# A cap on transfers under way, a planner that charges for instruction pages, and V scaled on VectorE in two groups

## The chip, the core and the metric

One core of a Trainium2 chip runs the whole program. Its engines work side by side, each through its own list of instructions in order: TensorE (PE in the profile; its weight loads are shown apart as PEld), VectorE (DVE), ScalarE (ACT), GpSimd (POOL) and SyncE (SP), which here issues the transfers between device memory and on-chip memory. An engine waits for another at a semaphore. The metric is the device time of one execution in microseconds (us), the median over runs.

## The reference

Two parts follow each other. The first is a delta-rule attention over 4 batches, 8 heads, 768 tokens and 48 dimensions, written token by token; the second is a gated MLP over the 3072 tokens that come out of it.

```python
k_n = k / (norm(k) + 1e-06)
for t in range(S):
    y[:, :, t] = q[:, :, t] @ state
    v_old = k_n[:, :, t] @ state
    state = state + beta[t] * outer(k_n[:, :, t], v[:, :, t] - v_old)
x = y as (3072, 384)
out = (sigmoid(x @ w_gate) * (x @ w_val)) @ w_out      # 384 -> 1536 -> 384
```

All values are float32.

## The kernel before

**Groups.** The 768 tokens are cut into 12 groups g of 64 tokens (all 32 pairs of batch and head at once). Inside a group the recurrence is not run token by token but solved: a Gram matrix of the keys (`gram`, L259), its blocks copied out by ScalarE (L267, L272), norms on VectorE (`norms`, from L208), then a triangular solve on VectorE, a row at a time. Groups 0 and 1 take a shorter solve on two halves (`solve_halves`, L343 and L346), after which TensorE joins the halves with two products of 128 small matmuls each, `pz` and `pm` (`joining`, L375), with a copy of z on ScalarE between them (`keep_z`, L379) and the step T on VectorE behind them (L355). The other groups use the long solve (L311, L314). Then the state's share is taken off V (`less`, L401), the updates are formed (`updates`, L413 and L420, copied by L426 and L428), the output rows (`rows`, L448 and L451) and, from them, the transposed input of the MLP (`flip`, L490; `keep_x`, L496 and L498). The next group's state comes from `advance` (L471, L478, L480). V is first scaled by the key norms, 16 operations of 48 elements on ScalarE for each group (`scale_v`, L247).

**MLP.** For each group and each of 12 blocks f of the hidden dimension there is a gate product of 18 matmuls (`gate_val`, L508), a sigmoid and a product (L513, L518), a split in an upper and a lower half (L523, L528), and an output product of 6 matmuls (`outp`, L544). Group 0 takes blocks 0 to 5 first, then group 1 takes all 12, then group 0 the rest, and after that each group has its 12 in turn.

**Weights.** They come as 36 pieces of 384 KB. Each is converted once: two operations on ScalarE (`tail_bits` L165, `rescale` L170), `join` on VectorE (L182), the upper half on ScalarE (L187) and the lower on VectorE (L192). All stay on the chip. The first six transfers go at once; piece n from 6 on waits for a one-element copy on GpSimd (`mark`, L175) that waits for the conversion of piece n - 6.

**Transfers.** All are issued by SyncE, in the planner's order: keys by dimension (`load_k`, L87), queries (`load_q`, L91), keys and V by token with beta (`load_rows`, L98, L101), pieces (`load_piece`, L155), and the stores of the results.

**The planner.** Every step is a task with an engine, a cost in ns, what it comes after, and the buffers that it takes and frees. `schedule` (from L751) gives each task a level, the longest way from it to the end, and builds the lists by a simulation: the engine that can start earliest takes the ready task of the highest level, with a small slack. Up to the first gate product it fills TensorE's gaps of over 450 ns with warm-up products of zeros (`warm_up`, L201), as many as it expects to fit; they are then fixed in the list. The order that comes out is each engine's program.

Of the kernel before, what the change touches and what calls it, by code (L numbers as in the profile page):

```python
# [14 lines left out]
U32 = mybir.dt.uint32  # L15
# [4 lines left out]
ALU = mybir.AluOpType  # L20
# [10 lines left out]
J = 8  # L31
CP = 2 * J
# [18 lines left out]
NSUB = GT // 128  # L51
EPS = 1e-6
CUT = 6


@with_exitstack
def deltanet_gated_mlp(ctx: ExitStack, tc: tile.TileContext, kd, qd, kv, beta, words, out):
# [24 lines left out]

    state = [{} for _ in range(N)]

    def load_k(g):
        for e in range(2):
            nc.sync.dma_start(kqp[g % 2][64 * e:64 * e + D, 0:2].rearrange("p s c t -> p (s c t)"), kd[g, e])  # L87

    def load_q(g):
        for e in range(2):  # L90
            nc.sync.dma_start(kqp[g % 2][64 * e:64 * e + 64, 2 + e:4 + e].rearrange("p s c t -> p (s c t)"), qd[g, e])  # L91

    def load_rows(g, part):

        st = state[g]
        if "kv" not in st:
            st["kv"] = wk.tile([128, 2, CP, D], F32, name=f"kv_{g}", tag="kv", bufs=2)
        nc.sync.dma_start(st["kv"][:, part].rearrange("p c d -> p (c d)"), kv[g, :, part * CP * D:(part + 1) * CP * D])  # L98
        if part:
            st["beta"] = wk.tile([128, 32], F32, name=f"beta_{g}", tag="beta", bufs=2)  # L100
            nc.sync.dma_start(st["beta"], beta[:, g])  # L101

    def load_group(g):
        load_k(g)
        load_q(g)
        load_rows(g, 1)
        load_rows(g, 0)

    def constants():
        nc.gpsimd.memset(zero, 0.0)  # L110
# [35 lines left out]
    pieces.append((NF - 1, "o"))  # L146
    raw, parts = {}, {}

    AHEAD = 6

    def load_piece(n):
        f, w = pieces[n]
        if n < AHEAD:
            raw[n] = wt.tile([128, PW, 2], U32, name=f"raw_{n}", tag=f"w{n}")
        nc.sync.dma_start(raw[n].rearrange("p c w -> p (c w)"), words[3 * f + "gvo".index(w)])  # L155

    def words_of(n):

# [8 lines left out]
    def rescale(n):  # L167

        h = words_of(n)[2].bitcast(F32)
        nc.scalar.activation(h, h, AF.Prelu, scale=2.0 ** -112, alpha=-2.0 ** 32)  # L170

    def mark(n):

        raw[n] = wt.tile([128, PW, 2], U32, name=f"raw_{n}", tag=f"w{n}")
        nc.gpsimd.tensor_copy(out=raw[n][0:1, 0:1, 0], in_=raw[n - AHEAD][0:1, 0:1, 1])  # L175

    us = {}

# [64 lines left out]

    def scale_v(g):
        V, mq = state[g]["kv"][:, 1], state[g]["mq"]
        for c in range(CP):
            nc.scalar.activation(V[:, c], V[:, c], AF.Copy, scale=mq[:, c, 0:1])  # L247
            yield
# [114 lines left out]
    def joining(g, n):  # L363

        st = state[g]
        if g == 0 and n == "pm":
            st["pm"] = st["pz"]
        else:
            pool, tag = (ps_aux, "aux") if g else (ps_gv, "gv")
            st[n] = pool.tile([128, CP, 32], F32, name=f"{n}_{g}", tag=tag)  # L370
        out = st[n]
        lhsT, rhs = (scratch[:, 0], mt) if n == "pz" else (scratch[:, 1], scratch[:, 2])
        for c in range(CP):
            for r in range(0, 128, 32):
                nc.tensor.matmul(out=out[r:r + 32, c], lhsT=lhsT[r:r + 32, c], rhs=rhs[r:r + 32, c], start=True, stop=True)  # L375

    def keep_z(g):

# [3 lines left out]
    def rest(g):  # L382

        st = state[g]
        kq, V = kqp[g % 2], st["kv"][:, 1]
# [6 lines left out]
        if g == 0:  # L392
            st["R"] = [V[:, e * J:(e + 1) * J] for e in range(2)]
        else:
            st["R"] = [None, None]

    def less(g, e, step):
# [5 lines left out]
    def updates(g, step):  # L403

        st = state[g]
        R, L = st["R"], st["L"]

        at = {(e, x): [tokens_at(e, x) + 32 * (k ^ e) for k in range(2)] for e, x in KINDS}
        if step == 1:
            for j in range(J):  # L410
                for e, x in KINDS:
                    one, two = at[e, x]
                    nc.tensor.matmul(out=st["pk"][e][two:two + 32, j], lhsT=L[one:one + 32, e * J + j], rhs=su[one:one + 32, 3 if x else e, j],  # L413
                                     start=False, stop=True, skip_group_check=True)
            return
        st["pu"] = pu = [ps_aux.tile([128, J, D], F32, name=f"pu_{g}_{step}_{x}", tag="aux") for x in range(1 if g else 2)]
        for j in range(J):
            for e, x in KINDS:
                r = at[e, x][step // 2]
                nc.tensor.matmul(out=pu[0 if g else x][r:r + 32, j], lhsT=mt[r:r + 32, e * J + j], rhs=R[e][r:r + 32, j], start=True, stop=True)  # L420
# [150 lines left out]
        tasks.append(t)  # L571
        return name

    def on_dve(n):
        return 158 + 1.03 * n

    def on_act(n):
        return 165 + 0.85 * n
# [15 lines left out]
    pools = dict(aux=2, seq=2, gv=1, po=2, G=1, gp=1, X=1, mt=1, scratch=1, row=3, ys=1, sg=3, h=3, u=3, kv=2, L=2, xa=0, xb=1, mq=1)  # L594
# [19 lines left out]
    def load(g, what):  # L614
        k = f"kq{g % 2}"
        if what == "k":
            transfer(f"dk{g}", lambda: load_k(g), 2, 1900, has(f"pk{g - 2}", f"pp{g - 2}"))
        if what == "q":
            transfer(f"dq{g}", lambda: load_q(g), 2, 2200, has(f"yy{g - 2}"))
        if what == "v":  # L620
            transfer(f"dv{g}", lambda: load_rows(g, 1), 2, 1350, has(f"pd{g - 2}", f"less{g - 2}.1.1"))
        if what == "t":
            transfer(f"dt{g}", lambda: load_rows(g, 0), 1, 1150, has(f"pd{g - 2}"))

    HALF = {0, 1}

    def recurrence(g):
# [12 lines left out]
        for i in range(4):  # L640
            by = [task(f"sv{g}.{i}", ACT, 1020, lambda: [next(sv, None) for _ in range(4)], by)]
# [32 lines left out]
        r = [f"sv{g}.3"]  # L674
        if g:
            r = [task(f"less{g}.0.{e}", DVE, 555, lambda e=e: less(g, e, 0), [f"pk{g}", f"sv{g}.3"], take=("row",)) for e in range(2)]
        kinds = [(e, x) for e, x in KINDS]
        two = g == 0

# [56 lines left out]

    half = constants()
    second_half(half)
    for n in range(len(pieces)):
        fetch(n)  # L740
        convert(n)
        split(n)
    for g in range(N):
        for what in "kvqt":
            load(g, what)
        recurrence(g)
    for i in range(N * NF):
        tile_of(i)
        out_of(i)

    def schedule():  # L751

# [3 lines left out]
            for a in t["after"]:  # L756
                a["then"].append(t)
        for t in reversed(tasks):
            t["level"] = t["late"] + max([(0 if b["engine"] == t["engine"] else LATENCY[t["engine"]] + t["lands"] + t["load"]) + b["level"] for b in t["then"]] or [0]) + t["cost"]
# [5 lines left out]
        order, between, filling = [], [], [True]  # L765

        def release(t):
            when[t["n"]] = max([a["done"] if a["engine"] == t["engine"] == PE else a["end"] for a in t["after"]] or [0.0])
# [4 lines left out]
        while len(order) < len(tasks):  # L773
# [19 lines left out]
            if e == PE and filling:  # L793
                clock[e] = max(clock[e], READY)
                while at - clock[e] > ROOM:
                    between.append(dict(name="warm", fn=warm_up, start=clock[e], engine=PE, done=clock[e] + FILL))
                    clock[e] += FILL
# [10 lines left out]
            clock[e] = t["done"]  # L808
            for p in t["free"]:
                tokens[p].append(t["end"])  # L810
            ready[e].remove(t)
            order.append(t)
            for b in t["then"]:
# [2 lines left out]
                    release(b)  # L816
        return sorted(order + between, key=lambda t: t["start"])

    READY, FILL, ROOM = 2500, 230, 450
# [51 lines left out]
```

## Time and profile before

| | before |
|---|---|
| Median of 3 runs | 655.1 us (653.84 to 655.85) |
| The profiled execution's own time | 654.68 us |
| Its span, first to last instruction | 652.6 us |
| TensorE busy | 630.2 us (97%) |
| VectorE busy | 475.4 us (73%) |
| ScalarE busy | 323.3 us (50%) |
| GpSimd busy | 16.6 us (3%) |
| Transfers, mean rate | 63 GB/s |

A line of groups names the line, the engine, the operation, what it writes and reads with shapes, and how often it comes; then its busy time and the mean length of one, and after the bar the idle time of the engine just before it and what ended that. "issue" means that the profile shows nothing that the engine waited for. A line of the timeline begins with the start and the length in us. TensorE's matmuls are pipelined, so a sum of lengths can exceed the time. The granted clock of TensorE is a share of its full speed.

### The profile page before, as it was taken

Reading aid. Unit: us, or ns where it says so; the run is one execution under the profiler, and the core shown is the slowest. Engines: PE = TensorE matmul, PEld = TensorE weight load, DVE = VectorE, ACT = ScalarE, POOL = GpSimd, SP = SyncE. Lnnn points to the kernel's source line nnn. Section 1 sums busy time; section 2 is a strip of 40 time slices with the busy share of each in tenths; the row PEclk is TensorE's granted clock in tenths of the full one; section 3 lists DMA queues with packets and bytes.
Section 4 is the critical chain, followed back from the end, with each engine's and each line's share of the span. In section 5 each row is a group of like instructions: output and inputs, shape, how many; then the busy total and the mean of one; then the engine's idle time right before and its main releaser. Section 6 shows DMA issues by size and latency. Waiting matters only on the chain.

```text
span 652.6 us, 24378 instructions
## 1 busy us (share of the span) xinstructions
PE 630.2 (97%) x10618; PEld 591.3 (91%) x10626; DVE 475.4 (73%) x1482; ACT 323.3 (50%) x881; POOL 16.6 (3%) x57
## 2 busy tenths in 40 slices
PE   8785999999999999999999999999999999999996
PEld 5445999989999999999999999999999999999996
DVE  4785799996977976976976976976976986983221
ACT  4867799346355355355345345345345345344321
POOL 5010100000000000000000000000000000000000
PEclk9988999999999999999999999999999999999999
DMA  9858350030211211211211211211211210100101
GB/s 262 267 182 268 110 160 12 2 83 20 58 51 28 58 52 27 58 51 27 59 52 27 58 51 28 59 51 27 58 51 28 59 51 3 27 2 4 25 1 24
DMA packets 17770, 41.08 MB, mean 63 GB/s; under 512 B 4224, under 2 KB 7296, under 8 KB 17664
## 3 DMA queue, kind: packets, MB, share of 16 engines
q1 hardware_dynamic: 17664, 39.53, 21.6%
q8 instruction: 83, 1.36, 0.9%
q14 instruction: 23, 0.19, 0.1%
HBM read 34.80 MB, written 4.72 MB: 61 GB/s over the span
## 4 chain that ended last, share of the span: by engine, by line
PE 85%; DMA 5%; DVE 4%; issue 3%; ACT 1%; SPq 0%; POOL 0%; ACTq 0%; POOLq 0%
PE gv L508 46%; PE po L544 23%; DMA raw<-in_words_dram 3%; PE pu L420 3%; PE yy L448 2%; PE yy L451 2%; PE pp L283 2%; PE pg L259 2%; PE pk L390 2%; PE pk L413 1%; DMA kv<-in_kv_dram 1%; PE pt L490 1%; PE pd L471 1%; DVE X L314 1%; DVE tmp L311 1%
## 5 line engine op out<-in xcount | busy, mean ns | idle before, releaser
L508 PE MATMUL gv<-xx,w 128*128 128x256 f32 x2592 | 333.1, 284 | 1.5 <-DVE sg L518 1.5
L508 PEld LDWEIGHTS gv<-xx,w 128*128 128x128 f32 x2592 | 325.6, 191 | 3.0 <-ACT sg L513 1.1
L544 PE MATMUL po<-w,h 128*128 128x384 f32 x864 | 180.7, 346 | 0.0
L544 PEld LDWEIGHTS po<-w,h 128*128 128x128 f32 x864 | 146.0, 188 | 3.8 <-ACT ot L556 0.2
L513 ACT ACTIVATE sg<-gv 128x256 f32<-128x256 f32 x144 | 54.9, 381 | 151.0 <-PE gv L508 150.7
L518 DVE TENSOR_TENSOR sg<-sg,gv 128x256 f32<-128x256 f32 x144 | 60.0, 416 | 78.8 <-ACT sg L513 78.6
L523 ACT CAST h<-sg 128x256 fp32r<-128x256 f32 x144 | 58.5, 406 | 89.6 <-DVE sg L518 88.9
L314 DVE TENSOR_TENSOR X<-X,tmp 128x126 f32<-128x126 f32 (+22 forms) x310 | 79.0, 255 | 9.1
L311 DVE TENSOR_TENSOR tmp<-X,gp 128x126 f32<-128x126 f32 (+22 forms) x310 | 78.2, 252 | 7.3
L528 DVE TENSOR_TENSOR h<-sg,h 128x256 fp32r<-128x256 f32 x144 | 59.9, 416 | 16.6 <-ACT h L523 15.9
L428 ACT COPY su<-pu 32x384 f32<-32x384 f32 x92 | 43.3, 471 | 23.8 <-PE pu L420 22.7
L247 ACT ACTIVATE kv<-kv,mq 128x48 f32<-128x48 f32 x192 | 46.9, 323 | 3.6 <-DVE mq L241 3.5
L201 PE MATMUL warm<-zero 128*128 128x512 bf16 x114 | 30.1, 420 | 3.9 <-issue 2.8
L288 DVE TENSOR_TENSOR kqp<-pp,pmask 64x512 f32<-64x512 f32 x48 | 32.1, 685 | 2.0 <-PE pp L283 1.7
L267 ACT COPY G<-pg 32x256 f32<-32x256 f32 (+1 forms) x72 | 26.4, 367 | 9.0 <-PE pg L259 5.4
L201 PEld LDWEIGHTS <-zero 128*128 128x128 bf16 x122 | 12.3, 106 | 17.8 <-issue 6.0
L208 DVE STREAM_TRANSPOSE gp<-G 128x1024 f32<-128x1024 f32 x12 | 14.9, 1245 | 16.8 <-ACT G L267 16.8
L401 DVE TENSOR_TENSOR R<-kv,pk 128x384 f32<-128x384 f32 x44 | 22.4, 550 | 3.3 <-PE pk L390 2.1
L192 DVE TENSOR_TENSOR w<-u,w 128x384 fp32r<-128x384 f32 x36 | 19.1, 552 | 5.3 <-ACT w L187 5.3
L480 DVE TENSOR_TENSOR su<-su,pd 48x384 f32<-48x384 f32 x40 | 22.1, 552 | 0.8
L187 ACT CAST w<-u 128x384 fp32r<-128x384 f32 x36 | 17.2, 511 | 6.1 <-DVE u L182 6.0
L420 PEld LDWEIGHTS pu<-R,mt 32*32 32x32 f32 x1408 | 16.4, 105 | 4.0 <-DVE R L401 2.3
(93 smaller groups left out, 464.0 us busy)
## 6 DMA issues: line engine op xcount, KB each, us to landing
raw<-in_words_dram SPq DMA_DIRECT2D x36, 384.0 KB, 6.1
kv<-in_kv_dram SPq DMA_DIRECT2D x24, 384.0 KB, 3.6
kqp<-in_qd_dram SPq DMA_DIRECT2D x24, 256.0 KB, 4.1
kqp<-in_kd_dram SPq DMA_DIRECT2D x24, 192.0 KB, 3.6
out_dram<-ot SPq DMA_DIRECT2D x48, 96.0 KB, 2.2
beta<-in_beta_dram SPq DMA_DIRECT2D x12, 16.0 KB, 3.7
```

Source lines behind the costliest of these rows:

```text
L201: nc.tensor.matmul(out=hot[0], lhsT=z.to_broadcast([128, 128]), rhs=z.to_broadcast([128, 512]), start=True, stop=True)
L247: nc.scalar.activation(V[:, c], V[:, c], AF.Copy, scale=mq[:, c, 0:1])
L311: nc.vector.tensor_tensor(out=tmp, in0=X[:, k:16, j:j + 1].to_broadcast([128, n, j]), in1=gp[:, j:j + 1, 0:j].to_broadcast([128, n, j]), o ...
L314: nc.vector.tensor_tensor(out=X[:, k:16, 0:j], in0=X[:, k:16, 0:j], in1=tmp, op=ALU.add)
L420: nc.tensor.matmul(out=pu[0 if g else x][r:r + 32, j], lhsT=mt[r:r + 32, e * J + j], rhs=R[e][r:r + 32, j], start=True, stop=True)
L428: nc.scalar.copy(su[r:r + 32, 3 if x else e], pu[0][r:r + 32])
L508: nc.tensor.matmul(out=pg[:, o], lhsT=parts[w, f][:, a, k * 128:(k + 1) * 128], rhs=x[b][:, k], start=(k == 0 and q == 0), stop=(k == KC - ...
L513: nc.scalar.activation(h, st["gv", f][:, 0], AF.Sigmoid)
L518: nc.vector.tensor_tensor(out=h, in0=h, in1=st["gv", f][:, 1], op=ALU.mult)
L523: nc.scalar.copy(hh[:, 0], st["sg", f])
L528: nc.vector.tensor_tensor(out=hh[:, 1], in0=st["sg", f], in1=hh[:, 0].bitcast(F32), op=ALU.subtract)
L544: nc.tensor.matmul(out=po[s], lhsT=hh[:, a, ts], rhs=parts["o", f][:, w], start=begins(g, f) and q == 0, stop=ends(g, f) and q == 2)
```

## The change

- `move` issues the transfers of a load. Its first one waits for the last one of the move two before (`FLIGHT = 2`). Stores do not go through it.
- The last matmul of group 0's `pm` is noted, and the first load that is issued after it in the planner's order waits for it. In the planner, pieces from 9 on (`HUSH = 9`), the queries of group 1 and the keys by token of group 1 come after `pm0`.
- The marks on GpSimd are gone: every piece has its own buffer from the start.
- For groups 0 and 1, `scale_v` is one VectorE operation of 768 elements a partition instead of 16 on ScalarE.
- The planner models the cap, TensorE at half speed until 12 us, the fetching of TensorE's instructions in pages of 256 (`paged`), and adds an urgency in ns (the table `URGENCY`) to the level of certain tasks. Warm-ups fill gaps of over 550 ns.

```diff
+FLIGHT = 2
+HUSH = 9
...
+    flown, calm = [], []
+
+    def move(pairs):
+
+        moves = [nc.sync.dma_start(to, of).ins for to, of in pairs]
+        for name in flown[-FLIGHT:][:len(flown) // FLIGHT and 1] + [calm.pop() for _ in calm[:1]]:
+            tc.add_manual_dep(moves[0], name, mybir.DependencyInfo(mybir.DependencyClass.Sync, mybir.DependencyReason.DATA), reason="transfers in flight")
+        flown.append(moves[-1].name)
...
     def load_piece(n):
         f, w = pieces[n]
-        if n < AHEAD:
-            raw[n] = wt.tile([128, PW, 2], U32, name=f"raw_{n}", tag=f"w{n}")
-        nc.sync.dma_start(raw[n].rearrange("p c w -> p (c w)"), words[3 * f + "gvo".index(w)])
+        raw[n] = wt.tile([128, PW, 2], U32, name=f"raw_{n}", tag=f"w{n}")
+        move([(raw[n].rearrange("p c w -> p (c w)"), words[3 * f + "gvo".index(w)])])
...
-    def mark(n):
-
-        raw[n] = wt.tile([128, PW, 2], U32, name=f"raw_{n}", tag=f"w{n}")
-        nc.gpsimd.tensor_copy(out=raw[n][0:1, 0:1, 0], in_=raw[n - AHEAD][0:1, 0:1, 1])
...
         V, mq = state[g]["kv"][:, 1], state[g]["mq"]
+        if g < 2:
+            nc.vector.tensor_tensor(out=V, in0=V, in1=mq[:, :, 0:1].to_broadcast([128, CP, D]), op=ALU.mult)
+            yield
+            return
...
+        if g == 0 and n == "pm":
+            calm.append(last.ins.name)
...
-        pre = []
-        if n >= AHEAD:
-            pre = [task(f"mark{n}", POOL, 170, lambda: mark(n), [f"rescale{n - AHEAD}"])]
-        transfer(f"w{n}", lambda: load_piece(n), 1, 1150, pre)
+        transfer(f"w{n}", lambda: load_piece(n), 1, 1150, has("pm0") if n >= HUSH else (), take=("flight",))
...
-            transfer(f"dq{g}", lambda: load_q(g), 2, 2200, has(f"yy{g - 2}"))
+            transfer(f"dq{g}", lambda: load_q(g), 2, 2200, has(f"yy{g - 2}", "pm0"), take=("flight",))
...
+    URGENCY = {"G1": 9500, "T2": -3000, "bits/21": 19000, "bits/30": 7000, "bits/33": -16000, "dk0": 48500, "dq1": -2000, "dt0": 12500, "h3": -2000, "hh1": 8000,
...
+               "u0": 5500, "w/21": 14500, "w/24": 21500, "w/3": 2000, "w/33": 11000, "whi/12": -500, "whi/15": -10000, "whi/30": 4500, "wlo/15": 1500, "wlo/18": -1000,
...
-        clock, moved = [0.0] * 5, [0.0]
+        clock, moved = [0.0] * 4 + [800.0], [0.0]
...
+        def paged(at, cost, words):
+
+            late = 0
+            for n in range(words):
+                p, now = (fetched[0] + n) % PAGE, at + late + cost * n / words
+                if p == TURN:
+                    late += max(0, fetched[1] - now)
+                if p == ASK:
+                    queued = moved[0] - now - 1000
+                    fetched[1] = now + 1900 + (0.35 * queued + 1350 if queued > 0 else 400)
+            fetched[0] += words
+            return late
...
-            cost = t["cost"]
+            cost = t["cost"] * (2 if e == PE and at < HOT else 1)
+            if e == PE:
+                cost += paged(at, cost, WORDS[t["name"].rstrip("0123456789.")])
...
+            if "flight" in t["take"]:
+                tokens["flight"].append(t["end"])
...
+    WORDS = dict(gram=129, pk=129, pp=129, pz=257, pm=256, u=128, yy=192, pd=128, pt=6, gate=36, out=12)
+    PAGE, ASK, TURN = 256, 6, 194
+    READY, HOT, FILL, ROOM = 2500, 12000, 230, 550
```

More of the change, by code (lines that the diff above doesn't have):

```diff
@@ L97, in load_rows @@
             st["kv"] = wk.tile([128, 2, CP, D], F32, name=f"kv_{g}", tag="kv", bufs=2)
-        nc.sync.dma_start(st["kv"][:, part].rearrange("p c d -> p (c d)"), kv[g, :, part * CP * D:(part + 1) * CP * D])
+        pairs = [(st["kv"][:, part].rearrange("p c d -> p (c d)"), kv[g, :, part * CP * D:(part + 1) * CP * D])]
         if part:
             st["beta"] = wk.tile([128, 32], F32, name=f"beta_{g}", tag="beta", bufs=2)
[L101 to L107, printed above, removed]
+            pairs.append((st["beta"], beta[:, g]))
+        move(pairs)
     def constants():
@@ L374, in joining @@
             for r in range(0, 128, 32):
-                nc.tensor.matmul(out=out[r:r + 32, c], lhsT=lhsT[r:r + 32, c], rhs=rhs[r:r + 32, c], start=True, stop=True)
+                last = nc.tensor.matmul(out=out[r:r + 32, c], lhsT=lhsT[r:r + 32, c], rhs=rhs[r:r + 32, c], start=True, stop=True)
+        if g == 0 and n == "pm":
+            calm.append(last.ins.name)
     def keep_z(g):
@@ L384, in rest @@
         st = state[g]
-        kq, V = kqp[g % 2], st["kv"][:, 1]
+        kq = kqp[g % 2]
         st["pk"] = pk = [ps_seq.tile([128, J, D], F32, name=f"pk_{g}_{e}", tag="seq") for e in range(2)]
@@ L391, in rest @@
                                  start=j == 0, stop=True, skip_group_check=True)
-        if g == 0:
-            st["R"] = [V[:, e * J:(e + 1) * J] for e in range(2)]
-        else:
+        if g:
             st["R"] = [None, None]
@@ L405, in updates @@
         st = state[g]
+        if g == 0 and "R" not in st:
+            st["R"] = [st["kv"][:, 1, e * J:(e + 1) * J] for e in range(2)]
         R, L = st["R"], st["L"]
@@ L572, in task @@
         return name
[L574 to L578, printed above, removed]
     LATENCY = {PE: 220, DVE: 30, ACT: 30, POOL: 60, SP: 0}
@@ L616, in load @@
         if what == "k":
-            transfer(f"dk{g}", lambda: load_k(g), 2, 1900, has(f"pk{g - 2}", f"pp{g - 2}"))
+            transfer(f"dk{g}", lambda: load_k(g), 2, 1900, has(f"pk{g - 2}", f"pp{g - 2}"), take=("flight",))
         if what == "q":
-            transfer(f"dq{g}", lambda: load_q(g), 2, 2200, has(f"yy{g - 2}"))
+            transfer(f"dq{g}", lambda: load_q(g), 2, 2200, has(f"yy{g - 2}", "pm0"), take=("flight",))
         if what == "v":
-            transfer(f"dv{g}", lambda: load_rows(g, 1), 2, 1350, has(f"pd{g - 2}", f"less{g - 2}.1.1"))
+            transfer(f"dv{g}", lambda: load_rows(g, 1), 2, 1350, has(f"pd{g - 2}", f"less{g - 2}.1.1"), take=("flight",))
         if what == "t":
-            transfer(f"dt{g}", lambda: load_rows(g, 0), 1, 1150, has(f"pd{g - 2}"))
+            transfer(f"dt{g}", lambda: load_rows(g, 0), 1, 1150, has(f"pd{g - 2}", *["pm0"] * (g == 1)), take=("flight",))
     HALF = {0, 1}
@@ L639, in recurrence @@
         by = [f"dv{g}", n[-1]]
-        for i in range(4):
-            by = [task(f"sv{g}.{i}", ACT, 1020, lambda: [next(sv, None) for _ in range(4)], by)]
+        for i in range(1 if g < 2 else 4):
+            by = [task(f"sv{g}.{i}", *((DVE, 950) if g < 2 else (ACT, 1020)), lambda: [next(sv, None) for _ in range(4)], by)]
+        scaled = by[0]
         by_name[by[0]]["free"] = ("mq",)
@@ L673, in recurrence @@
         by_name[m[3]]["free"] = (aux,)
-        r = [f"sv{g}.3"]
+        r = [scaled]
         if g:
-            r = [task(f"less{g}.0.{e}", DVE, 555, lambda e=e: less(g, e, 0), [f"pk{g}", f"sv{g}.3"], take=("row",)) for e in range(2)]
+            r = [task(f"less{g}.0.{e}", DVE, 555, lambda e=e: less(g, e, 0), [f"pk{g}", scaled], take=("row",)) for e in range(2)]
         kinds = [(e, x) for e, x in KINDS]
@@ L738, in deltanet_gated_mlp @@
     second_half(half)
[L739 to L742, printed above, removed]
     for g in range(N):
+        for n in range(len(pieces)):
+            if g == (n >= HUSH):
+                fetch(n)
+                convert(n)
+                split(n)
         for what in "kvqt":
@@ L749, in deltanet_gated_mlp, with urgency @@
         out_of(i)
+    URGENCY = {"G1": 9500, "T2": -3000, "bits/21": 19000, "bits/30": 7000, "bits/33": -16000, "dk0": 48500, "dq1": -2000, "dt0": 12500, "h3": -2000, "hh1": 8000,
[5 rows of a table added]
+    def urgency(name):
+        kind = name.split(".")[0]
+        word = kind.rstrip("0123456789")
+        number = kind[len(word):]
+        if word in ("w", "bits", "rescale", "join", "whi", "wlo"):
+            kind = f"{word}/{int(number) // 3 * 3}"
+        elif word in ("gate", "sig", "prod", "hh", "hl", "out"):
+            kind = f"{word}{int(number) // 6}"
+        return URGENCY.get(kind, 0)
     def schedule():
@@ L758, in schedule @@
         for t in reversed(tasks):
-            t["level"] = t["late"] + max([(0 if b["engine"] == t["engine"] else LATENCY[t["engine"]] + t["lands"] + t["load"]) + b["level"] for b in t["then"]] or [0]) + t["cost"]
-        clock, moved = [0.0] * 5, [0.0]
+            t["level"] = t["late"] + urgency(t["name"]) + max([(0 if b["engine"] == t["engine"] else LATENCY[t["engine"]] + t["lands"] + t["load"]) + b["level"] for b in t["then"]] or [0]) + t["cost"]
+        clock, moved = [0.0] * 4 + [800.0], [0.0]
         tokens = {p: [0.0] * n for p, n in pools.items()}
@@ L765, in schedule @@
         order, between, filling = [], [], [True]
+        fetched = [0, 0.0]
+        def paged(at, cost, words):
[9 more added lines that the diff above has]
+            return late
         def release(t):
@@ L795, in schedule @@
                 while at - clock[e] > ROOM:
-                    between.append(dict(name="warm", fn=warm_up, start=clock[e], engine=PE, done=clock[e] + FILL))
-                    clock[e] += FILL
+                    paged(clock[e], FILL, 2)
+                    took = FILL if clock[e] > HOT else 2 * FILL
+                    between.append(dict(name="warm", fn=warm_up, start=clock[e], engine=PE, done=clock[e] + took))
+                    clock[e] += took
                 if t["name"] == "gate0":
```

10 lines of the change are left out of this document (3 added, 7 removed), and 4 rows, old and new, of the table URGENCY.

## The prediction

> **What bounds the kernel now.** I read the page first, for its shares.
>
> ```profile
> span 652.6 us, 24378 instructions
> ...
> PE 630.2 (97%) x10618; PEld 591.3 (91%) x10626; DVE 475.4 (73%) x1482; ACT 323.3 (50%) x881; POOL 16.6 (3%) x57
> ...
> L201 PE MATMUL warm<-zero 128*128 128x512 bf16 x114 | 30.1, 420 | 3.9 <-issue 2.8
> ```
>
> TensorE is busy 97% of the span, and part of that is the 114 warm-up products (L201), which compute nothing and run ahead of the first gate product (L508). The change touches no matmul of the computation, so it can only alter how early TensorE gets useful work and how few holes remain. So I cut the span into stages, at the first gate product (62.2), the first one of group 1 (93.3), and where VectorE has caught up (150). Columns: TensorE, weight loads, VectorE, ScalarE, GpSimd (busy us, instructions), granted clock, DMA share, GB/s.
>
> ```profile
> 10.00:25.00 15.00, 14.84 (x181) 7.44 (x181) 13.28 (x57) 11.50 (x27) 1.23 (x7) 1.00 1.04 319
> 25.00:62.20 37.20, 25.04 (x797) 15.80 (x801) 25.66 (x79) 25.55 (x70) 3.43 (x16) 0.93 0.75 242
> 62.20:93.30 31.10, 30.49 (x695) 28.96 (x693) 25.48 (x55) 26.65 (x66) 2.50 (x7) 0.92 0.41 132
> 93.30:150.00 56.70, 54.58 (x682) 52.31 (x681) 52.56 (x157) 34.89 (x94) 0.94 (x2) 1.00 0.15 42
> ...
> 200.00:640.00 440.00, 440.00 (x7189) 426.40 (x7189) 317.36 (x1007) 196.03 (x548) 0.00 (x0) 1.00 0.14 37
> ```
>
> From 200 on TensorE has no gap and VectorE is at 317.36 / 440 = 72%: nothing to win. From 93.3 to 150 TensorE misses 56.7 - 54.58 = 2.1 us and VectorE is busy 52.56 / 56.7 = 93%. From 10 to 93.3 VectorE works 13.28 + 25.66 + 25.48 = 64.4 us of 83.3, or 77%, and is idle 18.9. It carries the triangular solves of groups 0 and 1 and two operations per weight piece, and without them no gate product may run. So the early part is VectorE's work, plus the holes in it; how many of the holes go is the whole question. The TensorE timeline shows the largest causes (start, length, then the idle time before it):
>
> ```profile
> 26.00 1.29 PE L375 MATMUL pz<-mt,scratch 32*32 32x32 f32 x128
> ...
> 28.19 0.38 PE L375 MATMUL pz<-scratch 32*32 32x32 f32 x23
> ...
> 32.01 1.09 PE L375 MATMUL pz<-scratch 32*32 32x32 f32 x105 [3.43 <-issue]
> ...
> 35.58 1.17 PE L420 MATMUL pu<-kv,mt 32*32 32x48 f32 x45 [0.17 <-issue]
> ...
> 55.83 1.25 PE L201 MATMUL warm<-zero 128*128 128x512 bf16 x5 [1.58 <-issue]
> 57.01 1.24 PE L375 MATMUL pz<-mt,scratch 32*32 32x32 f32 x123
> 62.03 0.32 PE L375 MATMUL pz<-mt,scratch 32*32 32x32 f32 x5 [3.78 <-issue]
> 62.27 4.21 PE L508 MATMUL gv<-xx,w 128*128 128x256 f32 x18
> 66.41 1.63 PE L375 MATMUL pm<-scratch 32*32 32x32 f32 x128
> ...
> 69.05 2.41 PE L508 MATMUL gv<-xx,w 128*128 128x256 f32 x18
> ```
>
> In both joinings (L375) TensorE stops in the middle of one task's matmuls for 3.43 and 3.78 us, with nothing to wait for ("issue"). The queue rows and two stretches say what that is:
>
> ```profile
> q8 instruction: 83, 1.36, 0.9%
> ...
> 24.00:28.00 4.00, 3.84 (x141) 2.22 (x140) 3.91 (x9) 2.91 (x11) 0.52 (x1) 1.00 1.03 340
> ...
> 32.00:36.00 4.00, 3.61 (x150) 2.31 (x154) 2.63 (x7) 0.00 (x0) 0.00 (x0) 0.65 0.02 4
> ...
> 56.00:60.00 4.00, 2.25 (x128) 1.44 (x127) 3.12 (x7) 2.22 (x10) 0.00 (x0) 1.00 1.06 261
> 60.00:64.00 4.00, 1.97 (x13) 1.91 (x13) 0.53 (x2) 1.55 (x4) 0.00 (x0) 0.56 0.78 259
> ```
>
> 10618 + 10626 instructions of TensorE over 83 packets is 256 each, and 1.36 MB / 83 is 16.4 KB: queue 8 carries TensorE's program, a page of 256 at a time. One joining product is 128 matmuls and 128 weight loads, a whole page in 1.3 us. Both long stops come with the DMA engines full (1.03, 1.06); the stop of 0.17 us, in a task that also eats pages fast, comes with them empty (0.02). I read the two long stops as pages held up behind data. After both the clock is low (0.65, 0.56): the first gate product takes 4.21 us against 2.41 for the second.
>
> **The change part by part.** The sum is made against the profiled execution: span 652.6, its own time 654.68, so 2.1 us outside the span; it lies 0.4 below the median 655.1. A gain in the span is taken from the median unchanged.
>
> *Joining of group 0.* Its transfers are held until its last matmul (the planner gives pieces from 9 on, q and the token keys of group 1 that edge, and the first later move waits for the matmul). The stop of 3.43 falls to something between 0.17 (the quiet row) and 3.43 (nothing helps). It is nearest to the quiet row, but two pages pass here and only half of one there; I take 0.8, a gain of 2.6. It is on VectorE's path, as these rows show:
>
> ```profile
> 33.20 0.69 DVE L355 TENSOR_TENSOR mt<-mt,pz 128x512 f32<-128x512 f32 x1 [3.76 <-issue]
> ...
> 63.48 1.03 DVE L192 TENSOR_TENSOR w<-u,w 128x384 fp32r<-128x384 f32 x2 [4.35 <-ACT w L187]
> ...
> 68.08 0.69 DVE L355 TENSOR_TENSOR mt<-mt,pm 128x512 f32<-128x512 f32 x1 [2.64 <-PE pm L375]
> ```
>
> The T step of group 0 stood 3.76 us, and all of group 1's norms behind it. **-2.6.**
>
> *Joining of group 1.* No hush here, only at most two moves under way. The stop lies between 0.17 and 3.78; with some data moving, I put it in the lower half at 1.5, a gain of 2.3. After 1.58 us of idling (the row at 55.83) the clock was still 1.00 in the stretch 56 to 60, so the slow matmuls go too: 4.21 - 2.41 = 1.8 and 1.63 - 1.29 = 0.3. VectorE stood 4.35 + 2.64 = 7.0 us behind this (the upper halves of the weights, L187, queue on ScalarE behind the copy of z; then T waits for pm), which covers the 4.4. **-4.4** (bounds 0 and -5.7, the latter with a stop of 0.17).
>
> *Order.* The planner charges for pages, counts TensorE at half speed up to 12 us, and adds urgencies: u0 +5500, dk0 +48500 and so on, which add up along a chain and lift all before it.
>
> ```profile
> 36.70 0.96 ACT L428 COPY su<-pu 32x384 f32<-32x384 f32 x2 [5.62 <-PE pu L420]
> ...
> 40.01 1.14 DVE L426 COPY su<-pu 32x384 f32<-32x384 f32 x2
> ...
> 42.91 0.88 PE L413 MATMUL pk<-su,L 32*32 32x48 f32 x64
> ...
> 55.16 1.02 DVE L498 TENSOR_TENSOR xx<-pt,xx 128x384 fp32r<-128x384 f32 x2 [1.31 <-ACT xx L496]
> ...
> DVE w L192 <- ACT w L187: 5.3, 2, 4.4
> ...
> DVE kv L401 <- PE pk L413: 0.8, 1, 0.8
> DVE ys L460 <- PE yy L451: 0.7, 1, 0.7
> ```
>
> Both engines copy the same products; ScalarE starts at 36.70, VectorE at 40.01, because group 1's norms were put first, and TensorE goes on at 42.91, after filling the hole with warm-ups beyond VectorE's end at 41.15. The chain of group 0 could be some 5 us shorter here. But VectorE was busy in it, so the norms only move behind: what comes back is its own idling for that chain. The row at 55.16 has 1.31; VectorE's waits up to 130 (the last three rows: total, times, longest) add 0.9 for the upper halves beside the long one, 0.8 and 0.7. I take half of these 3.7, since a new order has waits of its own. **-1.9** (0 to -5).
>
> *V of groups 0 and 1 on VectorE.* Removed from ScalarE: 32 of the 192 operations of L247, 46.9 / 192 = 0.244 us each, 7.8 us in two groups. Added on VectorE: two of 128x768.
>
> ```profile
> L247 ACT ACTIVATE kv<-kv,mq 128x48 f32<-128x48 f32 x192 | 46.9, 323 | 3.6 <-DVE mq L241 3.5
> ...
> L528 DVE TENSOR_TENSOR h<-sg,h 128x256 fp32r<-128x256 f32 x144 | 59.9, 416 | 16.6 <-ACT h L523 15.9
> ...
> L192 DVE TENSOR_TENSOR w<-u,w 128x384 fp32r<-128x384 f32 x36 | 19.1, 552 | 5.3 <-ACT w L187 5.3
> ```
>
> 256 elements cost 416 ns and 384 cost 552, so 768 cost 552 + 384 x 136/128 = 960 ns, an estimate. Both lie on the engine that bounds: **+1.9**. In group 0 it may fall into the wait before T, in which case it is +1.0. ScalarE's relief I count at nothing: from 10 to 93.3 it is busy 63.7 us of 83.3 (stretches above), less than VectorE; where it holds a chain, it is in the order term.
>
> *The marks.* Thirty GpSimd copies go, with the waits of the queue that issues transfers for them; in their place that queue waits for the landing two moves earlier, and whatever is queued behind (stores too) waits with it.
>
> ```profile
> SPq L155 <- POOL raw L175: 45.6, 18, 12.3
> ...
> raw<-in_words_dram SPq DMA_DIRECT2D x36, 384.0 KB, 6.1
> kv<-in_kv_dram SPq DMA_DIRECT2D x24, 384.0 KB, 3.6
> ...
> 133.04 1.22 PE L544 MATMUL po<-w,h 128*128 128x384 f32 x6
> ```
>
> The queue stood 45.6 us for marks already, so transfers were throttled before. A piece took 6.1 us in the crowd; a transfer of the same size 3.6 where mostly little else moves. Two under way give one per 1.8 to 3.05 us. From some 29 us on, 27 pieces, two held loads and four of group 2 are 33 moves: all landed by 29 + 59 = 88 to 29 + 101 = 130. The last piece is used by group 1's last output product, at 133 now and 7 earlier after. At the lower figure the cover is some 38 us: **0**. What it costs without that cover is the last rival.
>
> *Sum:* -2.6 - 4.4 - 1.9 + 1.9 = **-7.0**, then 655.1 - 7.0 = **648.1 us**. Stretches after 93.3 stay as they are (the same work, 93% of VectorE), shifted: the 2.1 us there may move by 1 either way. With the bounds of the joinings and the order, the forecast's own range is 645 to 651.5.
>
> **The rivals.**
>
> *The stops stay.* If the pages are late for another reason than data (the request comes too late, at 1.3 us a page), 3.43 and 3.78 stay with their slow clock. Left are order and V: -1.9 + 1.9 = 0, or at the order's better bound -5 + 1.9 = -3.1; in between, 653.5 to 652: I say **652.5**. For it: the quiet stop was in a task half as long. Against: it was twenty times shorter. [...]
>
> *VectorE packed as later.* The new order could fill 10 to 93.3 as densely as 93.3 to 150 already is: (64.4 + 1.9) / 0.927 = 71.5 in place of 83.3, a gain of 11.8: **643.3**. For it: the holes are 18.9 us and ScalarE is relieved. Against: group 0's chain alternates between three engines, and the second joining is not quiet.
>
> *Pieces land later than planned, and ScalarE stands at their head.* The plan gives a piece 2400 + 1150 ns from its issue and works in order; on ScalarE a conversion whose piece is not there holds every copy of the recurrence behind it. Two moves cost the plan 3.55 us; if they cost 3.6 plus an issue of 0.4, each move is late by (4.0 - 3.55) / 2 = 0.22 us, and this adds up, since each waits for one before: 15 moves ahead of the first joining and 33 after it, 48 x 0.22 = 10.6 us. Against the -7.0 that is +3.6: **658.7**. It decides above 7.0 / 48 = 0.15 us a move. For it: the 6.1 row, and the lost slack of pieces fetched far ahead. Against: the 3.6 row, and conversions run ahead of use, so that not all lateness reaches a chain.
>
> **How the numbers follow.** Forecast 0.48; stops stay 0.17; packed 0.20; late pieces 0.15. One measurement of this kernel tells 0.3%, 2.0 us, from no change: same is 653.1 to 657.1. Faster: nearly all of forecast and packed (0.67) and half of "stops stay" (0.09), 0.76. Same: the rest of that rival and the edges, 0.11. Slower: 0.13, of the late pieces. The range is 640 (packed, with no stop left) to 655.5 (stops stay and the order brings nothing); some 0.05 lies below and 0.14 above.
>
> **What would show it.** Right: idle before L375 with "issue" under 1 us in group 0 and under 2 in group 1; no stretch of 4 us after 30 with a clock under 0.9; the first gate product near 55 at 2.4 us; group 1's first near 86; VectorE at 83% or more from 10 to there; 27 GpSimd instructions; L247 x160. Wrong: stops of 3 us again (pages), ScalarE waiting for pieces for more than 5 us in all (the limit on transfers), or TensorE idle for more than 4 us between the first gate product and 150, which would mean that the early start was given back by VectorE.

## The result and the profile after

| | before | after |
|---|---|---|
| Median | 654.47 us (652.21 to 655.85, 4 runs) | 644.61 us (642.65 to 646.5, 4 runs) |
| Ratio, 95% interval | | 0.9852 (0.9811 to 0.9894) |
| Span of the profiled execution | 652.6 us | 643.0 us |

The kernel became faster by 9.9 us; 7.0 were forecast. In the spans it is 9.6 us, and the question is where they came from. First the stages of the kernel after, up to group 1's first gate product (at 86.1, in the kernel before at 93.1) and from there about as far as before; columns as in the prediction.

```profile
10.00:86.10 76.10, 63.38 (x1628) 49.31 (x1635) 66.06 (x191) 57.41 (x130) 0.53 (x1) 0.91 0.69 203
86.10:143.00 56.90, 56.71 (x705) 55.60 (x704) 53.27 (x164) 39.12 (x106) 0.00 (x0) 1.00 0.30 81
```

The same first stage of the kernel before, cut at that product's own start:

```profile
10.00:93.10 83.10, 70.17 (x1665) 52.01 (x1671) 64.24 (x188) 63.51 (x162) 7.15 (x29) 0.94 0.68 215
```

The first stage is 7.0 us shorter. VectorE works 66.06 - 64.24 = 1.8 us more in it and is idle 76.1 - 66.06 = 10.0 in place of 83.1 - 64.24 = 18.9. In the second stage TensorE's holes fell from 2.1 us (the row from 93.30 in the prediction) to 56.9 - 56.71 = 0.2. That makes 8.9. The other 0.7 are no holes: from that product to the end TensorE runs equally many matmuls in both kernels, and is busy 552.19 us with them before and 551.46 after. Why they take less is not shown.

TensorE's timeline of the kernel after, around the two joinings (start, length, idle time before; group 0's `pm` writes into the tile of its `pz` and bears that name in the trace):

```profile
25.03 1.28 PE L375 MATMUL pz<-mt,scratch 32*32 32x32 f32 x128 [2.02 <-DVE mt L351]
...
26.99 0.75 PE L375 MATMUL pz<-scratch 32*32 32x32 f32 x39
28.75 1.40 PE L375 MATMUL pz<-scratch 32*32 32x32 f32 x89 [1.01 <-issue]
30.48 0.63 PE L197 MATMUL warm<-zero 128*128 128x512 bf16 x1 [0.34 <-issue]
31.05 1.01 PE L422 MATMUL pu<-kv,mt 32*32 32x48 f32 x37
33.17 0.84 PE L422 MATMUL pu<-kv,mt 32*32 32x48 f32 x27 [1.12 <-issue]
...
52.81 2.39 PE L510 MATMUL gv<-xx,w 128*128 128x256 f32 x18
55.13 0.31 PE L375 MATMUL pm<-scratch 32*32 32x32 f32 x13
56.33 1.17 PE L375 MATMUL pm<-scratch 32*32 32x32 f32 x115 [0.88 <-issue]
57.43 1.71 PE L510 MATMUL gv<-xx,w 128*128 128x256 f32 x12
61.24 0.88 PE L510 MATMUL gv<-xx,w 128*128 128x256 f32 x6 [2.11 <-issue]
62.05 1.15 PE L392 MATMUL pk<-su,kqp 48*64 48x48 f32 x64
63.02 1.05 PE L283 MATMUL pp<-kqp 48*64 48x64 f32 x57
64.94 0.34 PE L283 MATMUL pp<-kqp 48*64 48x64 f32 x7 [0.87 <-issue]
```

Count instructions between the stops, two for each matmul: from the 39th of pm to the 37th of the update, 2 x (89 + 1 + 37) = 254; from the 13th of group 1's pm to the 12th of the gate product, 2 x (115 + 12) = 254; from there to the 57th of pp, 2 x (6 + 64 + 57) = 254. These stops lie a page of 256 apart (a few instructions are in no such row), whatever task lies there. Not every page brings one: between the stop in the update and the one in group 1's pm about four pages are used, three page ends among them without a stop. The trace also keeps when each packet of queue 8 moved. All five stops end 1.2 to 1.5 us after such a packet has landed (at 27.54, 31.69, 54.94, 59.99 and 63.48 us), and so do the two long ones of before (landed at 30.62 and 60.75, stops over at 32.01 and 62.03). The stops are shorter than before, at most 2.11 against 3.43 and 3.78, but there are five of them, and around the second joining 0.88 + 2.11 + 0.87 = 3.9 us in all, no less than the 3.78 of before. The clock did not fall around the second joining: the granted clock is 1.00 from 52.8 to 68, and the first gate product takes 2.39 us, against 4.21 before.

Of VectorE's and ScalarE's waits up to 130 us, those that answer to the ones shown of before (total, times, longest):

```profile
DVE R L401 <- PE pk L392: 2.6, 1, 2.6
...
DVE w L188 <- ACT w L183: 0.9, 1, 0.9
DVE kv L401 <- PE pk L415: 0.9, 1, 0.9
DVE su L428 <- PE pu L422: 0.8, 1, 0.8
```

```profile
ACT raw L166 <- DMA raw<-in_words_dram: 7.2, 10, 1.7
...
ACT raw L171 <- DMA raw<-in_words_dram: 2.9, 2, 1.6
```

The wait of 3.76 before T of group 0 is gone (the norms of group 1 now run around it), and of the 7.0 behind the second joining 2.6 + 0.9 = 3.5 are left. ScalarE now waits 10.1 us for pieces. Three rows of the page show the rest of the change:

```profile
PE 622.7 (97%) x10582; PEld 587.8 (91%) x10590; DVE 477.6 (74%) x1484; ACT 318.0 (49%) x849; POOL 9.0 (1%) x27
...
L247 ACT ACTIVATE kv<-kv,mq 128x48 f32<-128x48 f32 x160 | 39.0, 322 | 1.6 <-DVE mq L237 1.6
...
raw<-in_words_dram SPq DMA_DIRECT2D x36, 384.0 KB, 3.7
```

27 GpSimd instructions, 160 scalings on ScalarE, and a piece that lands in 3.7 us, not 6.1.

### The profile page after: what moved, and what is told of

It reads as the page before. It is cut to its first block, busy times and chain, and to the rows that moved or that the text cites. A ratio compares the mean times of both kernels' runs of the same rounds, so it can differ in the third digit from the quotient of the medians.

```text
span 643.0 us, 24155 instructions
## 1 busy us (share of the span) xinstructions
PE 622.7 (97%) x10582; PEld 587.8 (91%) x10590; DVE 477.6 (74%) x1484; ACT 318.0 (49%) x849; POOL 9.0 (1%) x27
## 4 chain that ended last, share of the span: by engine, by line
PE 87%; DVE 9%; issue 2%; POOL 1%; ACT 0%; ACTq 0%; DVEq 0%; POOLq 0%
PE gv L510 46%; PE po L546 24%; PE pu L422 3%; PE yy L453 2%; PE yy L450 2%; PE pp L283 2%; PE pk L392 2%; PE pk L415 2%; PE pg L259 2%; PE pd L473 1%; PE pt L492 1%; DVE X L314 1%; DVE tmp L311 1%; DVE H L346 1%; DVE tmp L343 1%
## 5 line engine op out<-in xcount | busy, mean ns | idle before, releaser
L247 ACT ACTIVATE kv<-kv,mq 128x48 f32<-128x48 f32 x160 | 39.0, 322 | 1.6 <-DVE mq L237 1.6
L197 PE MATMUL warm<-zero 128*128 128x512 bf16 x78 | 21.2, 418 | 2.9 <-issue 1.9
L166 ACT ACTIVATE raw<-raw 128x384 int32<-128x384 uint16 x36 | 19.9, 558 | 7.3 <-DMA raw<-in_words_dram 7.2
L171 ACT ACTIVATE raw<-raw 128x384 f32<-128x384 f32 x36 | 19.5, 551 | 2.9 <-DMA raw<-in_words_dram 2.9
L422 PE MATMUL pu<-R,mt 32*32 32x48 f32 x1408 | 19.8, 203 | 0.4 <-DVE kqp L288 0.4
```

## The experiments

Theory A is the prediction's: the stops are instruction pages held up by data; VectorE bounds the early part, and its idle time is what comes back. The rivals are in the texts on record. Times are medians of 4 to 10 runs; ratios are to the kernel before on the same chip. Each kernel has the trace of one execution only, and executions differ: in experiments 7, 8 and 11, which run the same order with the same waits up to about the first gate product, the stop in group 0's pm was 1.42, 1.68 and 1.76 us where the change's trace has 1.01, and that product came at 54.3, 54.0 and 53.6 us, not 52.8.

**1. The transfers without their waits, the order kept.**

```diff
-        for name in flown[-FLIGHT:][:len(flown) // FLIGHT and 1] + [calm.pop() for _ in calm[:1]]:
-            tc.add_manual_dep(moves[0], name, ...)
```

> The changed kernel with the waits of the transfers taken out, both the cap of two and the hush; every engine's order stays as it is. Theory A (the stops in the joinings are instruction pages that queue behind data): with all pieces issued at once the DMA engines are full up to 45 us, and the stops, which were 1.01 in pm of group 0, 1.12 in its first update, 0.88, 2.11 and 0.87 around the second joining, grow to 3 us and more in those that fall before 45 us, at the same places in the instruction list (254 to 256 instructions apart); the time rises by 3 to 6 us to 648 to 651. Rival B (the request of a page comes too late, data does not matter; the gain is the new order): stops of the same length, 643 to 646. Rival C (the cap costs more than it saves, since pieces arrive later): ScalarE no longer waits for pieces (10 us before 130) and the time falls below 643.

650.77 us, ratio 0.9944 (0.9916 to 0.9972): 6 us of the 10 are lost. TensorE's timeline of this kernel, two stretches of it, and one more row of the timeline:

```profile
27.16 0.54 PE L373 MATMUL pz<-scratch 32*32 32x32 f32 x39
33.10 1.40 PE L373 MATMUL pz<-scratch 32*32 32x32 f32 x89 [5.41 <-issue]
...
35.40 1.01 PE L420 MATMUL pu<-kv,mt 32*32 32x48 f32 x37
39.45 0.84 PE L420 MATMUL pu<-kv,mt 32*32 32x48 f32 x27 [3.04 <-issue]
```

```profile
28.00:36.00 8.00, 2.56 (x122) 2.00 (x125) 3.16 (x15) 1.47 (x3) 0.00 (x0) 0.63 1.04 270
...
62.00:70.00 8.00, 7.01 (x281) 6.60 (x280) 5.81 (x12) 6.84 (x18) 0.00 (x0) 1.00 0.02 4
```

```profile
67.37 0.86 PE L508 MATMUL gv<-xx,w 128*128 128x256 f32 x6 [0.99 <-issue]
```

The same two places, after the 39th and the 37th matmul; 5.41 and 3.04 us with the DMA engines full (share 1.04 from 28 to 36 us, 1.03 from 36 to 52), 1.01 and 1.12 with the waits (share 0.71 from 26 to 28 and 0.78 from 28 to 30 us, 0.64 from 32 to 34). Nothing else was changed, so data sets most of these lengths, and rival B falls; so does rival C. The packets say where the time goes: the page for the first of these stops begins to move at 29.93 us, 2.2 us after the stop has begun (1.5 us before it in the change), but takes 1.4 us to move, against 1.3. It is held up before it moves. The last stretch and the row behind it hold something new: around the second joining hardly any data moves (DMA share 0.02), and still a stop of 1.0 us is left. So a part of the stops is there without data, here where a page is used up in some 2.8 us (115 matmuls of pm and 12 of the gate product).

**2. The cap without the hush.**

```diff
-        for name in flown[-FLIGHT:][:len(flown) // FLIGHT and 1] + [calm.pop() for _ in calm[:1]]:
+        for name in flown[-FLIGHT:][:len(flown) // FLIGHT and 1]:
```

> The changed kernel without the hush, with the cap of two. Theory A: the stop in pm of group 0 grows from 1.01 to between 1.5 and 2.5, since two transfers now run through the joining (DMA share 0.7 and more in place of 0.62); the chain of group 0 is 0.5 to 1.5 us later; 644.5 to 646. If the cap is what matters and the hush does nothing: 644.6 within 0.5.

645.8 us, ratio 0.9878 (0.9837 to 0.992), which overlaps the interval of the change. The first stop did grow:

```profile
30.40 1.40 PE L375 MATMUL pz<-scratch 32*32 32x32 f32 x89 [2.38 <-issue]
```

2.38 us, against 1.01 to 1.76 in the four traces of this order with the hush. This trace is of the slowest of the four runs, 649.63 us. The hush seems to shorten that stop; that it makes the kernel faster is not shown. In this order the cap alone brings 5.0 of the 6.2 us that experiment 1 lost.

**3. The kernel before, in its own order, with cap and hush.**

```diff
+        for name in flown[-FLIGHT:][:len(flown) // FLIGHT and 1] + [calm.pop() for _ in calm[:1]]:
+            tc.add_manual_dep(moves[0], name, ...)
```

> The kernel before, in its own order and with its marks, with the cap and the hush added to its transfers. Theory A, by the terms of the prediction: the stop of 3.43 falls to about 1, the one of 3.78 to 1.5 or less, and no slow clock after it; 7 us of VectorE's idling shrink by 4 to 7; 648 to 651 against 654.5. If the new order is the whole gain: 654 within 1.5. If late pieces cost more (ScalarE stands behind them): over 655.

661.35 us, ratio 1.0105 (1.0074 to 1.0136): slower than before. The stops did what theory A says; TensorE's timeline:

```profile
30.12 1.91 PE L384 MATMUL pz<-scratch 32*32 32x32 f32 x128 [2.63 <-ACT scratch L390]
...
57.25 2.06 PE L459 MATMUL yy<-su,kqp 48*64 48x48 f32 x64 [11.31 <-ACT su L439]
...
68.52 0.25 PE L384 MATMUL pz<-mt,scratch 32*32 32x32 f32 x5 [1.24 <-issue]
```

No stop in pm of group 0, which here starts only after a wait of 2.63 us for the copy of z, so that its page, I take it, had that time to come; and 1.24 us in place of 3.78. But the output rows wait 11.31 us for a copy on ScalarE. ScalarE's timeline says why (some rows left out):

```profile
48.08 0.55 ACT L174 ACTIVATE raw<-raw 128x384 int32<-128x384 uint16 x1 [2.55 <-DMA raw<-in_words_dram]
...
55.67 0.54 ACT L179 ACTIVATE raw<-raw 128x384 f32<-128x384 f32 x1 [0.99 <-DMA raw<-in_words_dram]
56.23 0.96 ACT L439 COPY su<-pu 32x384 f32<-32x384 f32 x2
```

The copies stand behind conversions of pieces that the cap and the hush have made late. This is the prediction's last rival, late pieces at the head of ScalarE's queue, met in an order that did not know of the cap. In the changed order ScalarE waits 10.1 us for pieces too, but up to 150 us TensorE waits only 0.6 us for ScalarE.

**4. The urgencies at 0.**

```diff
-        return URGENCY.get(kind, 0)
+        return 0
```

> The changed kernel with every urgency at 0; the rest of the planner (pages, half speed, cap, hush) stays. Theory A (quiet transfers give most, the order 2 us): 646 to 648. Rival D (the order gives most of the gain): 650 to 654, with VectorE's idling from 10 us to group 1's first gate product back at 14 us or more in place of 10.0.

646.85 us, ratio 0.9894 (0.9862 to 0.9927). Its first stage:

```profile
10.00:86.60 76.60, 66.04 (x1645) 49.42 (x1650) 66.54 (x192) 57.78 (x132) 0.53 (x1) 0.93 0.70 202
```

VectorE is idle 76.6 - 66.54 = 10.1 us, as in the change. By the medians the urgencies give some 2 us, and the intervals overlap; rival D falls. The planner without them is enough for the early gain.

**5. V of groups 0 and 1 on ScalarE again.**

```diff
-            by = [task(f"sv{g}.{i}", *((DVE, 950) if g < 2 else (ACT, 1020)), ...
+            by = [task(f"sv{g}.{i}", ACT, 1020, ...
```

> The changed kernel with V of groups 0 and 1 scaled on ScalarE again (16 operations each), planned anew with the same urgencies. By the prediction's term (VectorE bounds the early part, its two operations cost 1.9 us there, ScalarE's 7.8 us lie beside): 642.5 to 644.5, a little faster. Rival (ScalarE's queue, which stands for pieces 10 us before 130, holds copies of the chain behind it): 647 to 650.

646.55 us, ratio 0.9878 (0.9825 to 0.9932). I had expected it a little faster; it is not, and it is not slower beyond the intervals either. The order is another one too, so this is one plan against another. TensorE has one wait that the change does not have:

```profile
PE yy L446 <- ACT su L426: 2.6, 1, 2.6
```

The output rows wait 2.6 us for a copy on ScalarE, where the scalings now run too; whether these hold the copy was not separated.

**6. Planned with pages at no cost.**

```diff
             fetched[0] += words
-            return late
+            return 0
```

> The changed kernel planned with pages at no cost; waits of the transfers, half speed until 12 us and urgencies stay. If the page model mostly places warm-ups: 645 to 647, stops of 1 to 2 us in both joinings as now. If it orders the joinings around the stops and that is worth much: over 648.

648.45 us, ratio 0.9908 (0.9877 to 0.9938), about 4 us above the change; its profiled execution was at the lower edge, 646.66. The first gate product comes at 57.3 in place of 52.8 us. In this plan too the edit comes with a new order.

```profile
DVE su L428 <- PE pu L422: 2.7, 2, 2.4
...
DVE mt L355 <- PE pz L375: 1.2, 1, 1.2
DVE mt L355 <- PE pm L375: 1.0, 1, 1.0
```

In these rows VectorE waits 4.9 us for tasks of TensorE, most of it where a stop lies in them or just ahead. The change has 0.8 for the updates and none for T, but 2.6 for pk, behind its stop of 2.11. All its waits for TensorE come to 4.5 us, and here to 5.5. In experiment 8, in the change's own order, T waits 1.7. So the waits mostly lie elsewhere; that the model of the pages orders work around the stops, and that this is worth the 4 us, is not shown.

**7. VectorE with more to do.**

```diff
-        nc.vector.scalar_tensor_tensor(out=u, in0=hi, scalar=3, in1=lo, ...)
+        for _ in range(2 if 2 <= n < 10 else 1):
+            nc.vector.scalar_tensor_tensor(out=u, in0=hi, scalar=3, in1=lo, ...)
```

> The changed kernel, every order as it is, where the join of pieces 2 to 9 is done twice on VectorE (the second time over itself): 8 more operations of 0.55 us, 4.4 us, between 48 and 72 us. If VectorE bounds the early part, nearly all of it shows: 647.5 to 649. If TensorE's own stops or the chain between engines bound it: less than 2 us, 644.6 to 646.6.

646.98 us, ratio 0.9886 (0.9842 to 0.9931). First stage:

```profile
10.00:88.60 78.60, 62.00 (x1637) 46.51 (x1636) 70.72 (x199) 57.58 (x130) 0.53 (x1) 0.98 0.72 206
```

The stage is 2.5 us longer than the change's 76.1 and VectorE's idle time fell from 10.0 to 7.9: about half of the 4.4 us went into holes. And 1.5 of the 2.5 us were there at the first gate product already, which none of the added work holds up. There the stops of this execution were longer, and one wait was new:

```profile
49.50 0.84 PE L493 MATMUL pt<-ident,ys 128*128 128x128 f32 x6 [2.59 <-ACT ys L465]
```

ScalarE stood 2.51 us for a late piece just ahead of that copy. So in this order too a late piece can hold the chain, in one execution and not in another.

**8. ScalarE with more to do.**

```diff
-        nc.scalar.copy(t[:, 0], us[n].bitcast(F32))
+        for _ in range(2 if 2 <= n < 10 else 1):
+            nc.scalar.copy(t[:, 0], us[n].bitcast(F32))
```

> The same for ScalarE: the upper half of pieces 2 to 9 is copied twice, 8 more operations of 0.51 us, 4.1 us, in about the same stretch. If VectorE alone bounds: 645 to 646.5. If ScalarE bounds as well (29.0 us busy of 33.3 between the first gate product and group 1's): 647.5 to 649.

646.43 us, ratio 0.9885 (0.9834 to 0.9936).

```profile
10.00:88.30 78.30, 66.98 (x1637) 49.64 (x1636) 66.63 (x192) 60.56 (x138) 0.53 (x1) 0.96 0.69 201
```

The stage grew by 2.2 us, of which 1.2 lay ahead of the first gate product. Past it, 4.4 us on VectorE and 4.1 on ScalarE each cost about 1 us. In the medians they cost 2.4 and 1.8 us, which the intervals do not tell from nothing. So neither engine alone bounds this part; I take it that chains that go to and fro between three engines do, with holes in each, but this is argued from the rest.

**9. Warm-ups in smaller gaps.**

```diff
-    READY, HOT, FILL, ROOM = 2500, 12000, 230, 550
+    READY, HOT, FILL, ROOM = 2500, 12000, 230, 230
```

> The changed kernel with warm-ups in every gap of over 230 ns (550 before), the rest planned alike. In the changed kernel the clock fell to 0.50 from 28 to 36 us and to 0.60 from 44 to 48, and the small matmuls of group 0's chain took some 2.5 us longer for it (1.40 for 89 of pm, 1.42 for 64 of pk, 1.95 for 32 of yy). If that delays the end: clock at 0.9 and more there, first gate product 1 to 2.5 us earlier, 642 to 644. If the chain has slack or warm-ups run into it: 644 to 647.

649.68 us, ratio 0.9937 (0.9913 to 0.9961). The clock was full in these stretches, and yet TensorE has a wait that was not there:

```profile
28.00:48.00 20.00, 16.40 (x486) 10.28 (x486) 18.00 (x63) 10.94 (x23) 0.00 (x0) 1.00 0.73 197
```

```profile
PE pu L422 <- DVE kqp L288: 3.2, 1, 3.2
```

The first gate product came 1.3 us earlier (51.5), but group 1's first 2.0 later: a new wait of 3.2 us of the updates for the masks appeared, and behind a stop of 1.73 us in pm a gate product took 3.85 us, not 2.40. The order changed with the warm-ups, so the clock's own worth is not isolated.

**10. A cap of three.**

```diff
-FLIGHT = 2
+FLIGHT = 3
```

> The changed kernel with a cap of three moves in the waits and in the planner. Theory A (pages queue behind data): stops of 1.5 to 2.5 us where there were 0.9 to 2.1, and ScalarE waits less for pieces (under 5 us before 130); the two about cancel, 643.5 to 647. If two cost more by late pieces than they save: below 643.

651.8 us, ratio 0.9966 (0.9948 to 0.9984). I expected a wash. The stops were short (0.56 and 1.01 us in group 0), so this is no case of late pages; in its order VectorE and TensorE wait for the upper halves on ScalarE, and TensorE has the wait for the masks of experiment 9:

```profile
DVE w L188 <- ACT w L183: 5.6, 3, 2.8
```

```profile
PE pu L422 <- DVE kqp L288: 3.2, 1, 3.2
PE gv L510 <- ACT w L183: 2.0, 1, 2.0
```

**11. A second hush, the order kept.**

```diff
-        if g == 0 and n == "pm":
+        if g < 2 and n == "pm":
```

> The changed kernel, every order as it is, where the first move issued after group 1's pm waits for its last matmul too. If data still sets the stops around the second joining (0.88, 2.11 and 0.87 us): together 2 us or less, 642.5 to 644. If pieces that come 2 to 4 us later cost as much: 644 to 647.

645.03 us, ratio 0.9867 (0.9826 to 0.9908): no difference from the change. A row of TensorE's waits, and the stretch of that stop:

```profile
PE gv L510 <- issue: 1.8, 1, 1.8
```

```profile
59.00:61.00 2.00, 0.15 (x2) 0.11 (x1) 1.52 (x4) 1.00 (x3) 0.00 (x0) 1.00 0.87 287
```

Two stops are left around the second joining, 1.85 and 1.14 us. The edit did not make the stretch quiet: the DMA share is 0.87. So whether quiet would help there is not tested, and a part of the stops is there without data, as in experiment 1.

**12. A second hush, planned.**

```diff
-        if g == 0 and n == "pm":
+        if g < 2 and n == "pm":
...
-        transfer(f"w{n}", ..., has("pm0") if n >= HUSH else (), take=("flight",))
+        transfer(f"w{n}", ..., has("pm0", "pm1") if n >= HUSH else (), take=("flight",))
```

The pieces from 24 on are made tasks after group 1's recurrence, so that the edge holds for them.

> As the second hush, but planned: pieces from 24 on come after group 1's pm in the planner too (with two edges that keep group 0's blocks and its lower left ahead of group 1's). If the second hush pays once it is planned: 641 to 643.5. If a new order loses what the urgencies were made for: 645 to 649.

647.94 us, ratio 0.9918 (0.9892 to 0.9943). Experiments 9, 10 and 12 all change one number or edge, get a new order with urgencies that were given for another one, and come out 3 to 7 us slower than the change; by its median the plan with no urgencies at all (experiment 4) beats the three. None of the kernels run here has a lower median than the changed one.

## Why the prediction was right, and where it was off

**The stops are pages behind data: right.** Their spacing of 254 instructions, the packets of queue 8 that land just ahead of their ends, and experiment 1 (5.41 us with the DMA engines full, 1.01 to 1.76 with the waits) show it. "The stops stay" is out for group 0, but that rival holds in part: some 1.0 us per stop is there without data.

**Joining of group 0, -2.6: right in size.** The stop in pm fell from 3.43 to 1.01 (to 1.76 at most in the other traces of this order), and T starts at 30.3 in place of 33.2, 2.9 us earlier. The rest of VectorE's 3.76 us was filled: V of group 0 and group 1's norms are now worked out there. I had not priced that the update behind it would get a stop of 1.12 (0.17 before).

**Joining of group 1, -4.4: about right in size, wrong in the way.** I let the stop shrink to 1.5; in sum it did not shrink (3.9 us in three places). What went is the slow clock (0.56 from 60 to 64 us before, 1.00 from 52.8 to 68 now) and half of VectorE's waiting, 7.0 to 3.5. The quiet floor of 0.17 that I used as a bound does not hold there: with hardly any data a stop of 1.0 remained in experiment 1. I misread the quiet row: its page had lasted 3.4 us (from 32.01 to 35.40), where the one ahead of the stop of 3.43 had lasted some 2.3 (from about 26.25 to 28.57), so it was not used up as fast.

**Order, -1.9, and V, +1.9: right as VectorE's account.** V shows as 1.8 us more busy time. The remaining idle time that went is 8.9 - 3.76 - 3.5 = 1.6. With that the first stage is 7.0 us shorter, as summed. That it meets the sum so closely is luck: the 1.6 is only what is left over, and with the same instructions up to there the first gate product comes up to 1.5 us later in other executions. Experiment 5 does not say that V on VectorE costs the kernel these 1.9 us; there the sign is open.

**"Stretches after 93.3 stay as they are": the step that failed.** It was to move by 1 us at most; TensorE's holes of 2.1 us closed to 0.2, and with 0.7 us less of TensorE's busy time, which nothing here explains, this is the rest of the gain in the spans. The new plan does it, and not the waits of the transfers. The second stage of experiment 1 (without the waits, at 92.0) and of experiment 3 (the old order with them, at 98.7):

```profile
92.00:150.00 58.00, 57.79 (x714) 56.69 (x713) 54.22 (x168) 39.49 (x107) 0.00 (x0) 1.00 0.08 22
```

```profile
98.70:155.60 56.90, 54.78 (x683) 52.51 (x682) 52.77 (x158) 35.14 (x95) 0.94 (x2) 1.00 0.19 54
```

TensorE's holes are 0.2 us in the one and still 2.1 in the other. In experiment 1 group 1's first gate product comes only 1.1 us earlier than before, and at the end the lead is 4.1. What in the plan closes the holes is open: without the urgencies 1.0 us is left, and with V on ScalarE again 2.0. I costed the order only by VectorE's waits up to the first stage.

**VectorE as the bound: too strong.** Its account adds up, but experiments 7 and 8 show that added work on it, or on ScalarE, is about half swallowed or more. "VectorE packed as later" did not come true either: 66.06 / 76.1 is 87%, not 93%. The time lies nearer to that rival's 643.3 than to the forecast's 648.1, but for another reason: most of the rest came past the first stage.

**Late pieces: right as a mechanism, and small in this kernel.** Experiment 3 pays for it 11.31 us in one wait; in the changed order experiment 7's execution had one of 2.59. My sign for it, more than 5 us of ScalarE waiting for pieces, was a bad one: the changed kernel waits 10.1 us and is the faster.

**The clock: wrong.** I expected no stretch after 30 us under 0.9, having seen a full clock after one gap of 1.58 us. It was at 0.50 from 28 to 36 us and at 0.60 from 44 to 48; see below.

The time of 644.6 us lies in the range, 0.4 us under the forecast's own of 645 to 651.5. That one is narrower than its bounds: added up, with VectorE's 1.9, they allow -12.1 to +1.9, or 643.0 to 657.0.

## What to carry to other kernels

Where an engine stops in the middle of a task with nothing to wait for, count its instructions between the stops and look at the DMA engines: here code came by a DMA queue too (queue 8, 83 packets of 16.4 KB), the stop for a page of it in group 0's pm was 5.41 us with the engines full and 1.01 with the cap and the hush, and capping the data was worth more than its earlier arrival (645.8 us with the cap alone against 650.77 without waits). Plan the order with the cap: the same waits made the order that was planned for them 6 us faster and the one that was not 7 us slower. And in this kernel a change of one planner constant gave a new order, so that it measured that order and not the constant.

## What the runs showed of the hardware

TensorE's granted clock fell to 0.50 with no hole of over 2.02 us ahead of it. In the kernel after:

```profile
23.30:26.70 3.40, 1.51 (x129) 1.31 (x130) 3.19 (x10) 2.33 (x5) 0.53 (x1) 1.00 0.74 231
26.70:37.00 10.30, 7.36 (x261) 5.17 (x262) 8.14 (x26) 4.75 (x10) 0.00 (x0) 0.50 0.64 187
```

The longest hole before the fall is the 2.02 us ahead of pz, with TensorE busy for 1.51 of the last 3.40 us, or about half with a warm-up whose record is missing, and then the clock is at 0.50 for 10 us. By the clock records of the two traces the stretches at 0.50 up to 70 us last 3.41 and 6.83 us in the kernel before, 10.24 and 3.41 in the one after; hence the 3.40 us here. In experiment 7, with the same instructions up to there, the gap was 1.48 us, and the clock fell only at about 35:

```profile
35.00:38.00 3.00, 3.00 (x69) 1.60 (x67) 2.23 (x5) 1.62 (x4) 0.00 (x0) 0.50 0.68 168
```

In experiment 11 TensorE was busy without a gap up to pz, and the clock fell at 29.3, in the stop of 1.76 us; there too TensorE had been busy for less than half (44%) of the 3.40 us before. So the moment differs between executions, and no single gap explains it.
